# A reciprocal and the low halves of m go ahead of block 0's products by denominators, and block 3's rows are loaded later

## The chip, the cores and the metric

The kernel runs on one core of a Trainium2 chip. A core has five engines, each with its own instruction queue, and an engine works through its queue strictly in the order in which the program was written: TensorE (PE) multiplies matrices and loads their weights (PEld), VectorE (DVE) and ScalarE (ACT) work elementwise, GpSimd (POOL) and SyncE (SP) mostly issue DMA transfers. An instruction that waits holds up everything behind it on its engine. The metric is the device time of one execution in microseconds (us).

## The reference

A transformer block on x of 2048 x 512 in float32, with a condition c that gives six vectors (shift, scale and gate for each half):

```python
mod = (_silu(c) @ w_mod)                 # sa, ca, ga, sb, cb, gb
h = layernorm(x) * (1 + ca) + sa
q, k, v = h @ wqkv                       # 32 heads of 16 columns
pq, pk = phi(q), phi(k)                  # phi(t) = (t > 0 ? t + 1 : exp(t)) + 1e-6
kv = einsum("bhsd,bhse->bhde", pk, v);  z = sum of pk over the rows
o = einsum(pq, kv) / (einsum(pq, z) + 1e-6)
x = x + ga * (o @ wo)
h = layernorm(x) * (1 + cb) + sb
x = x + gb * (mish(h @ w1 + b1) @ w2)    # 512 -> 1792 -> 512
```

## The kernel before, in words

The 2048 rows are cut into four blocks of 512, and a 512-wide dimension into four groups of 128 partitions. A product keeps float32 accuracy by splitting each operand into a high half (rounded, written `...h`) and a low half (the rest, `...l`); `mm3` then issues three matmuls, high x high, high x low, low x high. `split` makes the halves: ScalarE copies the high half, and one step later VectorE subtracts it to get the low half.

The part that the change touches lies at 120 to 200 us. There the keys are done, and the kernel makes q for blocks 2 and 3 and the attention output of all blocks:

- `q_unit(b, g)` multiplies 12 matmuls for group g of block b; `phi` then runs exp and relu on ScalarE and one combining instruction on VectorE (line 374).
- `attend(b, wait, ...)` is a generator that divides q of block b by its denominators. Step one: 16 small matmuls give the denominators (`den_b`, line 948). Step two: VectorE adds a constant and takes the reciprocal (`rden_b`, lines 952 and 953), and a DMA queue writes it to DRAM and reads it back spread over the partitions (`rd_b_0` to `rd_b_3`, lines 955 and 959; for blocks 0 and 1 from POOL's queue, for 2 and 3 from SP's). Then `wait` empty steps. Then, for two pairs of groups, VectorE multiplies q by `rd` (line 967), ScalarE makes the high half, and a step later VectorE makes the low half: `qs_b_gh` and `qs_b_gl`.
- m is the 512 x 512 product of kv and wo, as four products `m_ps_k` whose halves are `m_kh` and `m_kl`.
- `o_unit(b, t)` multiplies 12 matmuls: for g = 0 to 3 the halves of `qs_b_g` with those of `m_g`; `o_post` (line 987) adds the result to the rows of x that `load_x(b, t, "r")` fetched from SP's queue.
- `mod_side` loads columns of the modulation weights (`wm_i`, on SP) and three steps later reduces each on VectorE (line 254). SP also loads pieces of w1 and w2 (`w1p`, `w2p`) and stores prepared operands of w2 (`w2t`) for the second half of the kernel.

The order is set by the code alone here. Side work is spawned as a generator, and `tick()` runs one step of each spawned generator, in the order in which they were spawned. `tick()` is called once after each unit of TensorE, so that a step's instructions stand in the engines' queues behind that unit. From about 194 us on a planner with estimated costs sets the order of the second half of the kernel. Tiles come from one pool of 93 buffers; a load waits until the last reader of the buffer's former tile is done.

## Time and profile before

| | |
|---|---|
| median of three executions | 479.73 us |
| lowest, highest | 479.22, 481.56 us |
| profiled execution, its own time | 481.74 us |
| span of the profile, first to last instruction | 480.0 us |
| mean granted TensorE clock | 0.996 |
| busy: TensorE, VectorE, ScalarE, GpSimd | 470.1, 419.8, 325.6, 150.4 us |

The profiled execution is one of its own, with 1.7 us of its time outside the span. A row of the timeline gives start, duration, engine, line, operation, output <- inputs and the count; in brackets the time for which the engine stood idle before it and what released it. Names in the trace lack block numbers: `qs_2h` is group 2, and the block follows from the time.

### The profile page before, as it was taken

What the parts mean: (1) busy time and instruction counts of PE and PEld (TensorE: products, weight loads), DVE (VectorE), ACT (ScalarE), POOL (GpSimd) and SP (SyncE); (2) the same over time, 40 slices, a digit from 0 to 9 for tenths busy, and PEclk for the clock granted to TensorE, in tenths of its full rate; (3) what the DMA queues carried; (4) which work ended last, traced back from release to release, by engine and by line L of the source; (5) the groups of instructions that cost most, each with busy time, mean ns of one, the idle gap of its engine ahead of it and who ended that gap; (6) DMA issues with size and microseconds to landing.
All of it is one profiled execution on the core that took longest, in us unless ns stands there. A gap on an engine that the chain in (4) does not pass through costs nothing.

```text
span 480.0 us, 7249 instructions
## 1 busy us (share of the span) xinstructions
PE 470.1 (98%) x2292; PEld 385.9 (80%) x2292; DVE 419.8 (87%) x816; ACT 325.6 (68%) x593; POOL 150.4 (31%) x220
## 2 busy tenths in 40 slices
PE   8999999999998999999999999999999999999996
PEld 6788888878876888888888888888888887788886
DVE  6989999898989998998989899989876767999974
ACT  6777686776753998679979898576466657456330
POOL 4583431000022413224342221622131325607330
PEclk9999999999998999999999999999999999999999
DMA  8997699434996466348899542984352469999967
GB/s 308 402 352 213 179 184 269 136 111 133 325 262 165 142 222 215 119 154 273 251 310 320 183 136 83 196 265 133 109 154 66 114 196 231 246 301 191 262 105 131
DMA packets 80480, 97.76 MB, mean 204 GB/s; under 512 B 29521, under 2 KB 53081, under 8 KB 80442
## 3 DMA queue, kind: packets, MB, share of 16 engines
q1 hardware_dynamic: 54376, 57.82, 38.9%
q0 software_dynamic: 22752, 38.43, 32.5%
q10 hardware_dynamic: 3314, 1.05, 1.0%
q8 instruction: 18, 0.29, 0.3%
q14 instruction: 20, 0.16, 0.1%
HBM read 69.22 MB, written 31.99 MB: 211 GB/s over the span
## 4 chain that ended last, share of the span: by engine, by line
PE 88%; DVE 4%; DMA 3%; ACT 2%; issue 1%; POOL 0%; ACTq 0%; POOLq 0%; DVEq 0%
PE p_a L1565 20%; PE pa L1650 11%; PE p_s L1565 8%; PE pc L1650 5%; PE pb L1650 4%; PE pd L1650 4%; PE o L144 3%; PE o L142 3%; PE o L143 3%; PE pq_a L488 3%; PE pk L143 2%; PE gacc L142 2%; PE pk L142 2%; PE pk L144 2%; PE gacc L143 2%; PE gacc L144 2%
## 5 line engine op out<-in xcount | busy, mean ns | idle before, releaser
L1580 ACT ACTIVATE u<-p_a 128x512 f32<-128x512 f32 x42 | 25.0, 596 | 30.3 <-PE p_a L1565 29.7
L1524 POOL DMA_DIRECT2D wt_m<-w2t x32 | 27.9, 1096 | 55.3 <-PE p_a L1565 13.4
L1589 ACT ACTIVATE u_a<-c_a,b1c 128x512 f32<-128x512 f32 x42 | 30.2, 719 | 14.7 <-DVE c_a L1586 12.8
L1715 POOL DMA_DIRECT2D out_dram<-turned x20 | 23.3, 1719 | 36.2 <-DVE turned L1703 24.6
L1586 DVE TENSOR_TENSOR c_a<-p_s,u 128x512 f32<-128x512 f32 x28 | 19.3, 689 | 15.5 <-PE p_s L1565 8.0
L1539 DVE TENSOR_TENSOR u_a<-u_a,u_a 128x512 f32<-128x512 f32 x28 | 18.6, 682 | 0.0
L983 POOL DMA_DIRECT2D out_dram<-r x16 | 9.0, 562 | 27.7 <-DVE r L987 14.9
L278 POOL TENSOR_TENSOR rs_n<-rs_n,half 128x1 f32<-128x1 f32 x16 | 10.6, 667 | 19.7 <-DVE rs_n L304 9.8
L955 POOL DMA_DIRECT2D rden_d<-rden x2 | 1.4, 721 | 47.1 <-DVE rden L953 47.1
L1524 POOL DMA_DIRECT2D wt_m<-w2d x13 | 12.8, 1228 | 10.8 <-DVE c_a L1586 5.0
L371 ACT ACTIVATE e_k<-pk 128x512 f32<-128x512 f32 x15 | 8.9, 591 | 10.5 <-PE pk L144 10.4
L1681 ACT ACTIVATE U<-pa,mc 128x512 f32<-128x512 f32 x10 | 6.9, 686 | 11.1 <-PE pa L1650 11.0
L967 DVE SCALAR_TENSOR_TENSOR q<-q,rd 128x512 f32<-128x512 f32 x16 | 10.6, 686 | 3.9 <-DMA rd<-rden_d 3.9
L1586 DVE TENSOR_TENSOR c_a<-p_a,u 128x512 f32<-128x512 f32 x14 | 9.6, 687 | 4.2 <-PE p_a L1565 1.7
L374 DVE SCALAR_TENSOR_TENSOR ku<-e_k,relu_k 128x512 f32<-128x512 f32 x15 | 10.7, 714 | 2.9 <-ACT relu_k L372 2.7
L278 POOL TENSOR_TENSOR rs_x<-rs_x,half 128x1 f32<-128x1 f32 (+1 forms) x10 | 7.9, 792 | 15.8 <-DVE rs_x L273 14.6
L1617 ACT ACTIVATE u_a<-p_a,b1c 128x512 f32<-128x512 f32 x14 | 9.6, 687 | 4.5 <-PE p_a L1565 4.4
L1366 POOL DMA_DIRECT2D w1p<-w1d x13 | 9.9, 764 | 7.9 <-PE p_a L1565 3.5
L374 DVE SCALAR_TENSOR_TENSOR q<-e_q,relu_q 128x512 f32<-128x512 f32 x16 | 10.6, 686 | 0.5 <-ACT relu_q L372 0.5
L254 DVE SCALAR_TENSOR_TENSOR wm<-wm,sc_row 128x512 f32<-128x512 f32 x16 | 10.6, 678 | 0.0
L1342 ACT ACTIVATE l_m_0h<-u_a 128x512 fp32r<-128x512 f32 x12 | 7.5, 623 | 4.1 <-DVE u_a L1539 4.1
L1348 DVE TENSOR_TENSOR l_m_1l<-u_a,l_m_1h 128x512 fp32r<-128x512 f32 x12 | 8.2, 685 | 2.0 <-ACT l_m_1h L1342 2.0
(1446 smaller groups left out, 1879.4 us busy)
## 6 DMA issues: line engine op xcount, KB each, us to landing
wt_m<-w2t POOLq DMA_DIRECT2D x32, 256.0 KB, 4.4
wt_m<-w2t SPq DMA_DIRECT2D x22, 256.0 KB
r<-in_x_dram SPq DMA_DIRECT2D x16, 256.0 KB
out_dram<-r POOLq DMA_DIRECT2D x16, 256.0 KB, 3.3
x<-in_x_dram SPq DMA_DIRECT2D x15, 256.0 KB
wt_m<-w2d SPq DMA_DIRECT2D x15, 256.0 KB
w1d<-in_w_dram SPq DMA_DIRECT2D x4, 896.0 KB
w1p<-w1d SPq DMA_DIRECT2D x13, 256.0 KB
```

What stands on the lines that cost most here:

```text
L142: pe.matmul(o, st[0], mv[0], start=start, stop=False)
L143: pe.matmul(o, st[0], mv[1], start=False, stop=False)
L144: pe.matmul(o, st[1], mv[0], start=False, stop=stop)
L374: dve.scalar_tensor_tensor(dst, e, 1.0, r, op0=ALU.min, op1=ALU.add)
L1524: q.dma_start(f32(v), (w2d if src == "w2d" else w2t)[g][:, :, part, :])
L1539: dve.tensor_tensor(get(d), u, v, op=o)
L1565: pe.matmul(p, st, mv, start=onto is None and c == 0 and i == 0, stop=c == 1 and i == 2, skip_group_check=onto is not None)
L1580: act.activation(t["u", n], t["pa"], AF.Copy)
L1586: dve.tensor_tensor(t[key], t[p], t["u", n], op=ALU.add)
L1589: act.activation(u, t[key], AF.Mish, bias=b1c[:, f:f + 1])
L1650: pe.matmul(o, st[:, cs], mv, start=not onto and n == 0 and k == 0, stop=n == G - 1 and k == 2, skip_group_check=onto)
L1715: q.dma_start(rows_, sq, accum_op=ALU.add)
```

## The change

On VectorE, in the third unit of q for block 2, block 0's products by denominators come later. `attend(0)` has one empty step less, but is spawned one unit later, after m's splits and behind `attend(1)`. Its second pair of products no longer waits a step for the low halves (`join`). `mod_side` takes its first step by hand at the place where it was spawned, so that its loads keep their step, and runs on behind `attend(0)`. The four loads of block 3's rows go from the units of q for block 2 to the output units of block 0.

```diff
-    def attend(b, wait, queue=pool):
+    def attend(b, wait, queue=pool, join=False):
...
             next(parts[-1])
             if g % 2:
-                yield
+                if g == 1 or not join:
+                    yield
                 run(parts.pop(0))
                 run(parts.pop(0))
...
-    attending = attend(0, 3)
+    attending = attend(0, 2, join=True)
     next(attending)
...
     for g in range(4):
         q_unit(2, g)
-        if g == 1:
-            spawn(attending)
         if g == 2:
             spawn(attend(1, 4))
         if g == 1:
-            spawn(mod_side(range(12, 16), 1))
-        load_x(3, g, "r")
+            mods = mod_side(range(12, 16), 1)
+            next(mods)
         if g == 2:
             for k in range(4):
                 m_ps = ps("acc", f"m_ps_{k}")
                 mm3(m_ps, [h[:, P * k:P * (k + 1)] for h in kvs[0]], wos[k], True, True)
                 spawn(split(f"m_{k}", m_ps, ms, k))
+            spawn(attending)
+            spawn(mods)
         tick()
...
             for t in range(4):
+                load_x(3, t, "r")
                 o_unit(0, t)
```

The first place is VectorE's queue around `rden_1`, from the last of the `mod` columns on. `q_b_g` is q of block b and group g. Before:

```order
L967 SCALAR_TENSOR_TENSOR q_0_0_1380<-q_0_0_1380,rd_0_0_1631 128x512
L967 SCALAR_TENSOR_TENSOR q_0_1_1406<-q_0_1_1406,rd_0_1_1633 128x512
L374 SCALAR_TENSOR_TENSOR q_2_2_1727<-e_q_2_2_1756,relu_q_2_2_1757 128x512
L952 TENSOR_SCALAR rden_1_1819<-den_1_1760,tiny_den_525 128x128
L953 RECIPROCAL rden_1_1819<-rden_1_1819 128x128
L156 TENSOR_TENSOR m_0l_1778<-m_ps_0_1730,m_0h_1777 128x512
L156 TENSOR_TENSOR m_1l_1781<-m_ps_1_1734,m_1h_1780 128x512
L156 TENSOR_TENSOR m_2l_1784<-m_ps_2_1738,m_2h_1783 128x512
L156 TENSOR_TENSOR m_3l_1787<-m_ps_3_1742,m_3h_1786 128x512
L156 TENSOR_TENSOR qs_0_0l_1810<-q_0_0_1380,qs_0_0h_1809 128x512
L156 TENSOR_TENSOR qs_0_1l_1814<-q_0_1_1406,qs_0_1h_1813 128x512
```

And the same place in the changed kernel:

```order
L374 SCALAR_TENSOR_TENSOR q_2_2_1723<-e_q_2_2_1748,relu_q_2_2_1749 128x512
L952 TENSOR_SCALAR rden_1_1801<-den_1_1752,tiny_den_525 128x128
L953 RECIPROCAL rden_1_1801<-rden_1_1801 128x128
L156 TENSOR_TENSOR m_0l_1770<-m_ps_0_1724,m_0h_1769 128x512
L156 TENSOR_TENSOR m_1l_1773<-m_ps_1_1728,m_1h_1772 128x512
L156 TENSOR_TENSOR m_2l_1776<-m_ps_2_1732,m_2h_1775 128x512
L156 TENSOR_TENSOR m_3l_1779<-m_ps_3_1736,m_3h_1778 128x512
L967 SCALAR_TENSOR_TENSOR q_0_0_1380<-q_0_0_1380,rd_0_0_1631 128x512
L967 SCALAR_TENSOR_TENSOR q_0_1_1406<-q_0_1_1406,rd_0_1_1633 128x512
L156 TENSOR_TENSOR qs_0_0l_1820<-q_0_0_1380,qs_0_0h_1819 128x512
L156 TENSOR_TENSOR qs_0_1l_1824<-q_0_1_1406,qs_0_1h_1823 128x512
```

The first two products moved behind seven instructions that use no `rd`. The second place follows directly on VectorE, with the second pair of products. Before:

```order
L967 SCALAR_TENSOR_TENSOR q_0_2_1474<-q_0_2_1474,rd_0_2_1635 128x512
L967 SCALAR_TENSOR_TENSOR q_0_3_1481<-q_0_3_1481,rd_0_3_1637 128x512
L254 SCALAR_TENSOR_TENSOR wm_12_1712,mc_147<-wm_12_1712,sc_row_148 128x512
L374 SCALAR_TENSOR_TENSOR q_2_3_1802<-e_q_2_3_1836,relu_q_2_3_1837 128x512
L156 TENSOR_TENSOR qs_0_2l_1862<-q_0_2_1474,qs_0_2h_1861 128x512
L156 TENSOR_TENSOR qs_0_3l_1866<-q_0_3_1481,qs_0_3h_1865 128x512
```

And in the changed kernel:

```order
L967 SCALAR_TENSOR_TENSOR q_0_2_1474<-q_0_2_1474,rd_0_2_1635 128x512
L967 SCALAR_TENSOR_TENSOR q_0_3_1481<-q_0_3_1481,rd_0_3_1637 128x512
L156 TENSOR_TENSOR qs_0_2l_1862<-q_0_2_1474,qs_0_2h_1861 128x512
L156 TENSOR_TENSOR qs_0_3l_1866<-q_0_3_1481,qs_0_3h_1865 128x512
L254 SCALAR_TENSOR_TENSOR wm_12_1698,mc_147<-wm_12_1698,sc_row_148 128x512
L374 SCALAR_TENSOR_TENSOR q_2_3_1796<-e_q_2_3_1828,relu_q_2_3_1829 128x512
```

The low halves now stand directly behind their products, and `wm_12` and `q_2_3` behind them. On ScalarE only one row moves: the copy `gb_row` (4 x 128) goes from behind `qs_0_3h` to ahead of `qs_0_2h`. TensorE's and POOL's orders stay as they were. The third place is SP's queue, which loads block 3's rows (`r_3_t`). Before, they stand between the loads of `wm_17` and `wm_14`:

```order
L167 DMA r_3_0_1659<-in_x_dram 128x512
L178 DMA wm_18_1661<-wmd_68 128x512
L178 DMA wm_19_1663<-wmd_68 128x512
L167 DMA r_3_1_1700<-in_x_dram 128x512
L178 DMA wm_12_1712<-wmd_68 128x512
L167 DMA r_3_2_1728<-in_x_dram 128x512
L843 DMA w2t_3_1748<-t0_3h_1639 128x512
L843 DMA w2t_3_1748<-t0_3l_1640 128x512
L843 DMA w2t_3_1748<-t1_3h_1642 128x512
L843 DMA w2t_3_1748<-t1_3l_1643 128x512
L178 DMA wm_13_1754<-wmd_68 128x512
L167 DMA r_3_3_1803<-in_x_dram 128x512
```

In the changed kernel they are gone from there and stand here:

```order
L178 DMA wm_15_1870<-wmd_68 128x512
L167 DMA r_3_0_1898<-in_x_dram 128x512
L852 DMA w1p_1_0_1916<-w1d_526 128x4x128
L852 DMA w1p_1_1_1917<-w1d_526 128x4x128
L167 DMA r_3_1_1920<-in_x_dram 128x512
L167 DMA r_3_2_1969<-in_x_dram 128x512
L955 DMA rden_d_2_2004<-rden_2_2001 4x32x128
L959 DMA rd_2_0_2006<-rden_d_2_2004 128x1x512
L959 DMA rd_2_1_2008<-rden_d_2_2004 128x1x512
L959 DMA rd_2_2_2010<-rden_d_2_2004 128x1x512
L959 DMA rd_2_3_2012<-rden_d_2_2004 128x1x512
L167 DMA r_3_3_2015<-in_x_dram 128x512
```

So three of them moved to either side of the `w1p` loads, ahead of `rden_2`'s store, and the last behind block 2's `rd`.

## Prediction

> **What bounds the kernel now.** I read the page's busy times first, then the waits of TensorE, then busy time by stage with the granted clock, then the instructions of one stage engine by engine.

> ```profile
> span 480.0 us, 7249 instructions
> PE 470.1 (98%) x2292; PEld 385.9 (80%) x2292; DVE 419.8 (87%) x816; ACT 325.6 (68%) x593; POOL 150.4 (31%) x220
> PE o L144 <- DVE qs_2l L156: 1.0, 1, 1.0
> PE o L142 <- ACT qs_2h L150: 0.6, 1, 0.6
> ```

> TensorE is the bound: it is busy for 98% of the span. So a change gains only where TensorE stands still or runs slowly. The list of its waits is short, and two of its longest belong to one product: o(0,0), the first output product of block 0, waits for the high and then for the low half of `qs_2`. Does it also cost clock? The next table shows two stretches of 3.41 us there, and a later one in which TensorE also stands still for about a microsecond (first column the stretch, last three the granted clock, the share of DMA and its GB/s).

> ```profile
> core 0: us, PE busy (x) PEld busy (x) DVE busy (x) ACT busy (x) POOL busy (x), PEclk, DMA share, GB/s
> 148.10:151.51 3.41, 1.77 (x7) 1.01 (x7) 3.41 (x8) 3.29 (x7) 1.57 (x3) 1.00 0.09 11
> 151.51:154.92 3.41, 3.41 (x10) 2.64 (x9) 3.41 (x10) 0.01 (x1) 1.32 (x3) 0.50 0.90 220
> 407.50:410.92 3.42, 2.47 (x12) 1.77 (x10) 3.42 (x7) 3.34 (x7) 0.00 (x0) 1.00 1.23 273
> ```

> TensorE is busy for only 1.77 of 3.41 us (52%) in the stretch with the waits, and the stretch after it runs at a clock of 0.50. Around 409 us it was busy for 72% of such a stretch, and the clock stayed at 1.00. So the stall is paid twice: as idle time, and as half speed behind it. Its exact price stands in TensorE's instructions:

> ```profile
> 147.90 0.39 PE L144 MATMUL o<-m_1h,qs_1l 128*128 128x512 f32 x1
> 148.90 0.50 PE L142 MATMUL o<-m_2h,qs_2h 128*128 128x512 f32 x1 [0.61 <-ACT qs_2h L150]
> 150.66 0.50 PE L144 MATMUL o<-m_2h,qs_2l 128*128 128x512 f32 x1 [1.02 <-DVE qs_2l L156]
> 155.81 0.39 PE L144 MATMUL o<-m_3h,qs_3l 128*128 128x512 f32 x1
> 160.01 0.39 PE L142 MATMUL o<-m_0h,qs_0h 128*128 128x512 f32 x1
> 162.50 0.39 PE L144 MATMUL o<-m_3h,qs_3l 128*128 128x512 f32 x1
> ```

> From the start at 147.90 to the start at 155.81 lie 18 matmuls (the rest of o(0,0), 6, and all 12 of o(0,1)). An undisturbed product of 12 matmuls, o(0,3), goes from 160.01 to 162.50 in 11 steps, 0.227 us each. 18 steps are 4.09 us; 7.91 us passed. The loss is **3.82 us**. The half clock is 3.41 x 0.5 = 1.71 us of it; the waits are the other **2.11 us**.

> Why are the halves of `qs_2` late? VectorE tells it:

> ```profile
> 138.41 0.17 DVE L258 TENSOR_SCALAR mc<-mc 128x4 f32<-128x4 f32 x1
> 140.60 0.69 DVE L967 SCALAR_TENSOR_TENSOR q<-q,rd 128x512 f32<-128x512 f32 x1 [2.03 <-DMA rd<-rden_d]
> 141.50 0.69 DVE L967 SCALAR_TENSOR_TENSOR q<-q,rd 128x512 f32<-128x512 f32 x1 [0.21 <-DMA rd<-rden_d]
> 142.12 0.68 DVE L374 SCALAR_TENSOR_TENSOR q<-e_q,relu_q 128x512 f32<-128x512 f32 x1
> 142.72 0.34 DVE L952 TENSOR_SCALAR rden<-den,tiny_den 128x128 f32<-128x128 f32 x1
> 143.97 0.63 DVE L156 TENSOR_TENSOR m_0l<-m_ps,m_0h 128x512 fp32r<-128x512 f32 x1
> 146.30 0.68 DVE L156 TENSOR_TENSOR qs_0l<-q,qs_0h 128x512 fp32r<-128x512 f32 x1
> 147.50 1.28 DVE L967 SCALAR_TENSOR_TENSOR q<-q,rd 128x512 f32<-128x512 f32 x2
> 148.71 0.68 DVE L254 SCALAR_TENSOR_TENSOR wm<-wm,sc_row 128x512 f32<-128x512 f32 x1
> 149.92 0.68 DVE L156 TENSOR_TENSOR qs_2l<-q,qs_2h 128x512 fp32r<-128x512 f32 x1
> ```

> VectorE has no idle time before any row from 142.12 to 149.92, but ahead of that it stands still for 2.03 + 0.21 = 2.24 us, waiting for the denominators that a DMA spreads, while seven instructions that need no denominator (`q_2_2`, two for `rden_1`, four low halves of m) are queued behind. Later two instructions that block 0 doesn't need (`wm`, `q_2_3`) stand between the products and `qs_2l`.

> **The change, part by part.** (1) On VectorE the seven instructions go ahead of the products; nothing is added. Where their inputs come from:

> ```profile
> 137.29 1.08 PE L948 MATMUL den<-q,hmask 128*32 128x128 f32 x32
> 134.77 0.59 ACT L372 ACTIVATE relu_q<-pq 128x512 f32<-128x512 f32 x1
> 137.40 0.60 ACT L150 ACTIVATE m_3h<-m_ps 128x512 fp32r<-128x512 f32 x1
> 141.39 0.63 ACT L150 ACTIVATE qs_0h<-q 128x512 fp32r<-128x512 f32 x1 [3.40 <-DVE q L967]
> 148.22 0.63 ACT L150 ACTIVATE qs_2h<-q 128x512 fp32r<-128x512 f32 x1 [4.38 <-DVE q L967]
> L959 POOL DMA_DIRECT2D rd<-rden_d x4: 604/613/636, 133.6 to 135.4; - x4
> DMA to landing us min/median/max: 7.0/8.1/10.4
> ```

> `den_1` ends at 138.37, the rectified `q_2_2` at 135.36, the last high half of m at 138.00: all are there when VectorE is free at 138.58. The walk through the new order, with the steps of the rows above: `q_2_2` 0.60 to 139.18; `rden_1` and its reciprocal 1.25 (142.72 to 143.97) to 140.43; four low halves 2.33 (143.97 to 146.30) to 142.76. The products then need `rd_0` and `rd_1`, which landed by 140.60 and 141.50: they are hidden, 1.21 for two (147.50 to 148.71), to 143.97. ScalarE starts a high half 0.79 behind its product's start (140.60 to 141.39): `qs_0h` runs 143.55 to 144.18, so VectorE waits some 0.25 us, then two low halves to 145.4, and the second pair of products to 146.65.

> (2) Their low halves follow in the same step. `qs_2h` starts 0.79 behind 145.4, ends at 146.85; `qs_2l` runs from about 146.95 to 147.6, `qs_3l` to 148.2. TensorE, undisturbed, wants them at 147.90 + 0.23 = 148.13 (`qs_2h`), 148.58 (`qs_2l`) and 149.27 (`qs_3l`), and loads weights one step earlier. Margins: 1.0, 0.75 and 0.8 us. So both waits go, and with 100% busy stretches the half clock too: **-3.82 us** at o(0,1)'s end. If the estimate of the chain is wrong by more than 0.75 us, each further microsecond costs one.

> (3) What goes behind: `wm_12` and `q_2_3` come behind `qs_3l`, to start at 148.2 and 148.8, before 148.71 and 149.32. `q_2_3` feeds `den_2`, which TensorE would reach at 156.13 - 3.82 = 152.3: 2.8 us to spare. ScalarE has the exponential and the rectifier of `q_2_3` (0.59 each) between `qs_1h` and `qs_2h`, and now `gb_row` too, a row of four partitions that I take at no more than half of that: from 144.8 it ends at 146.2 at the latest, and `qs_2h` starts at 146.2. All this costs nothing, and what covers it are these margins.

> (4) The four loads of block 3's rows (256 KB each) leave SP's queue among the `wm` loads; three now stand behind `wm_15`, one behind block 2's `rd`. Issue time of those `rd`, and the rows' first reader:

> ```profile
> 163.86 2.89 SPq L959 DMA_DIRECT2D rd<-rden_d  x4
> 199.24 0.68 DVE L1861 TENSOR_TENSOR r<-o,r 128x512 f32<-128x512 f32 x1
> ```

> The latest of the four is so issued near 167, and with the slowest landing above (10.4 us) it is there by 178, 21 us early: nothing. What they stood ahead of on SP comes earlier: the `wm` tiles, four `w2t` stores, the `w2p` and `w1p` loads. These meet the transfer of `rd`. At 273 GB/s, the rate of the stretch at 407 us, where DMA is full, a load takes 0.96 us and four take 3.8. Bounds for the last landing of block 0's `rd`, now 135.4 + 10.4 = 145.8: 3.8 earlier (four loads gone from ahead of it) to 3.8 later (as much brought in). `q_0_3` wants it at 146.05. I take "the same or earlier", since what is removed stood ahead of `rd`, and what comes instead waits for tiles that computation frees. Three of the four also stand ahead of `rden_2`'s store on SP, which issues some 3 us before 163.86; they would have to be 12 us late to hold it up.

> (5) Does the gain last? VectorE gains 2.24 - 0.25 = 2.0 us, TensorE 3.8, so VectorE falls 1.8 us behind. What TensorE asks next:

> ```profile
> 161.70 0.68 DVE L156 TENSOR_TENSOR qs_3l<-q,qs_3h 128x512 fp32r<-128x512 f32 x1
> 162.93 0.69 DVE L987 TENSOR_TENSOR r<-o,r 128x512 f32<-128x512 f32 x1 [0.41 <-PE o L144]
> 168.17 0.39 PE L142 MATMUL o<-m_0h,qs_0h 128*128 128x512 f32 x1
> 171.09 0.69 DVE L987 TENSOR_TENSOR r<-o,r 128x512 f32<-128x512 f32 x1 [0.91 <-PE o L144]
> 181.64 0.68 DVE L156 TENSOR_TENSOR qs_3l<-q,qs_3h 128x512 fp32r<-128x512 f32 x1
> 183.69 0.39 PE L144 MATMUL o<-m_3h,qs_3l 128*128 128x512 f32 x1
> 160.00:180.00 20.00, 20.00 (x116) 16.29 (x115) 17.91 (x40) 18.64 (x38) 5.61 (x10) 1.00 0.65 209
> ```

> Block 1's last half is done at 162.4, and o(1,0) starts at 168.17: 5.8 us of cover for a lag of 1.8. VectorE itself waited 0.41 and 0.91 us for TensorE; those 1.32 us vanish, so by 171 the lag is some 0.5 us. In block 2 the cover is thin: `qs_3l` ends at 182.3, wanted at 183.69, 1.4 us less the weight load; it holds for 0.5 (without it, 0.5 us more to pay). ScalarE is busy for 18.64 us of the 20 from 160 on, so it makes up 1.36 us of the same lag; what is left, some 0.5 us, is inside that cover too. Behind this the order is fixed and whatever waits moves along. I carry -3.8 to the end, with 1 us as the most that may be lost here.

> **The sum.** The profiled execution took 481.74 us (span 480.0): 481.74 - 3.82 = 477.9. But the other executions took 479.22, 479.73 and 481.56. Two of them are 2.0 and 2.5 below the profiled one, one equals it within 0.2: a difference of the size of the half clock (1.71). I read it so: the half clock comes in some executions, not in others, and in the median one it did not come. Then the median loses only the waits: 479.73 - 2.11 = **477.6**, near 477.9. If the median did contain it, 479.73 - 3.82 = 475.9. [...]

> **Rivals.**
> *The half clock has another cause.* For it: a gap of 0.95 us near 409 drew none. Against: 52% busy just ahead of it, and the full clock in the other rows shown. Then the profiled time falls by 2.11 only, to 479.6. [...]
> *Part of the wait stays:* the chain product, high half, low half is longer than my steps by 1.5 us, so `qs_2l` stops TensorE for 0.75 and more. No half clock at 1 us (the stretch at 409). About 478.6.
> *It does nothing:* the wait only goes from `qs_2` to `qs_0`, as the products start 2.2 us later (142.76 against 140.60). Against: `qs_0l` ended at 146.98 before and ends near 144.9 now. 479.7.
> *Slower:* `rd_3` of block 0 lands later, as the brought-forward `w2p`, `wm` and `w1p` loads share its DMA engines, and the second pair of products waits for it with everything else queued behind. From a landing at 146.8 (146.05 plus the margin) it stops TensorE, one to one. With the half clock behind such a stall, it is as dear as the old wait at 146.8 + 3.82 - 1.71 = 148.9, and at my bound, 149.6, it costs 2.8 + 1.71 = 4.5 us where the median before paid 2.11: 482.1. For it: 10.4 us to landing is already the longest of the `rd`. Against: the margins in (4).

> **How the numbers follow.** No change means within 0.5% (2.4 us), about what a measurement can tell here. Waits gone, no half clock in the median before: 0.47, 477.6 (its own range 476.9 to 478.3, so a third of it below 477.33). Waits gone and half clock with them, against the median: 0.31, 475.9. Another cause of the half clock: 0.04, 477.6 to 479.6. Part stays: 0.07. Nothing: 0.05. Slower: 0.06, of it 0.05 beyond 0.5%. Faster by over 0.5%: 0.31 + 0.16 = 0.47; slower 0.05; the rest, 0.48, within. The range goes from 475.5 (the second case with 0.4) to 479.2 (part stays with half a microsecond).

> **What would show it.** Right: `q_2_2`, `rden_1` and m's low halves from 138.6 on without a wait before them; no TensorE wait at `qs_2h` or `qs_2l`; clock 1.00 from 145 to 160; `den_2` near 152.3. Wrong: a DMA wait at the second pair of products; a wait of TensorE at block 2's `qs` that was not there; a half-clock stretch elsewhere; `o` of block 3 waiting for its rows.

## The result, and the profile after

The changed kernel takes 477.99 us (median of nine executions, 477.15 to 479.07), the kernel before, beside it, 480.68 us (nine, 479.22 to 482.38). The ratio is 0.9944 with a 95% interval of 0.9924 to 0.9964: 0.56% faster. The interval leaves out 1, but reaches into the 0.5% that the prediction counts as no change. The profiled execution of the changed kernel took 477.43 us.

The page of the changed kernel, its span, the busy times and the chain of work that ended last; the fourth line is that chain in the kernel before:

```profile
span 475.7 us, 7248 instructions
PE 468.3 (98%) x2292; PEld 385.0 (81%) x2292; DVE 419.8 (88%) x816; ACT 325.1 (68%) x593; POOL 150.6 (32%) x220
PE 93%; DVE 3%; issue 1%; DMA 1%; ACT 1%; POOL 0%; ACTq 0%; DVEq 0%
PE 88%; DVE 4%; DMA 3%; ACT 2%; issue 1%; POOL 0%; ACTq 0%; POOLq 0%; DVEq 0%
```

VectorE does as much as before (419.8 us); TensorE's part of the chain has grown from 88 to 93%: before, the chain ran over DMAs and VectorE from 128 to 151 us, and now it is back on TensorE from 135 us on. TensorE's waits in the changed kernel (engine, line, what was waited for: us in total, times, longest):

```profile
PE warm L213 <- POOL ones L205: 1.1, 1, 1.1
PE tp_x L622 <- ACT x L287: 0.9, 1, 0.9
PE pc L1652 <- DVE l_m_5l L1350: 0.3, 1, 0.3
PE gacc L425 <- POOL pk_2h L152: 0.2, 1, 0.2
```

Both waits at `o` are gone. VectorE's timeline shows the new order (start, duration, engine, line, operation):

```profile
138.80 0.69 DVE L374 SCALAR_TENSOR_TENSOR q<-e_q,relu_q 128x512 f32<-128x512 f32 x1
139.40 0.34 DVE L952 TENSOR_SCALAR rden<-den,tiny_den 128x128 f32<-128x128 f32 x1
139.78 0.95 DVE L953 RECIPROCAL rden<-rden 128x128 f32<-128x128 f32 x1
140.65 0.63 DVE L156 TENSOR_TENSOR m_0l<-m_ps,m_0h 128x512 fp32r<-128x512 f32 x1
...
142.99 1.28 DVE L967 SCALAR_TENSOR_TENSOR q<-q,rd 128x512 f32<-128x512 f32 x2
144.37 0.69 DVE L156 TENSOR_TENSOR qs_0l<-q,qs_0h 128x512 fp32r<-128x512 f32 x1
...
145.58 1.29 DVE L967 SCALAR_TENSOR_TENSOR q<-q,rd 128x512 f32<-128x512 f32 x2
146.96 0.69 DVE L156 TENSOR_TENSOR qs_2l<-q,qs_2h 128x512 fp32r<-128x512 f32 x1
147.57 0.69 DVE L156 TENSOR_TENSOR qs_3l<-q,qs_3h 128x512 fp32r<-128x512 f32 x1
```

No row names a wait (some 0.1 us of idle time is left ahead of `qs_0l` and of `qs_2l`), where the kernel before stood 2.24 us for `rd`. TensorE now runs through the place; this is its timeline, and one stretch of 8 us with the busy time of TensorE, weight loads, VectorE, ScalarE and GpSimd, then the granted clock, the DMA share and GB/s:

```profile
148.44 0.39 PE L142 MATMUL o<-m_2h,qs_2h 128*128 128x512 f32 x1
148.67 0.39 PE L143 MATMUL o<-m_2l,qs_2h 128*128 128x512 f32 x1
148.90 0.39 PE L144 MATMUL o<-m_2h,qs_2l 128*128 128x512 f32 x1
149.12 0.39 PE L142 MATMUL o<-m_3h,qs_3h 128*128 128x512 f32 x1
...
152.62 1.08 PE L948 MATMUL den<-q,hmask 128*32 128x128 f32 x32
148.00:156.00 8.00, 8.00 (x63) 6.36 (x62) 8.00 (x18) 4.17 (x10) 2.97 (x6) 1.00 0.55 145
```

The steps are 0.227 us throughout, the clock is 1.00, and `den_2` comes at 152.62 instead of 156.13.

**Where the time went.** I set the starts of all 2292 matmuls of the two profiled executions side by side. Up to 148 us the changed one is 0.3 us later, from the start of the kernel on. Between 148 and 156 us it gains 3.85 us, and keeps this until 406 us, where another 0.75 us is added at a weight tile of the second half (see the last experiments). In sum 4.31 us, the difference of the two executions' times.

### The profile page after: what moved, and what is told of

Same layout as the page of the kernel before. It is cut to its first block, busy times and chain, and to the rows that moved or that the text cites. A ratio compares the mean times of both kernels' runs of the same rounds, so it can differ in the third digit from the quotient of the medians.

```text
span 475.7 us, 7248 instructions
## 1 busy us (share of the span) xinstructions
PE 468.3 (98%) x2292; PEld 385.0 (81%) x2292; DVE 419.8 (88%) x816; ACT 325.1 (68%) x593; POOL 150.6 (32%) x220
## 4 chain that ended last, share of the span: by engine, by line
PE 93%; DVE 3%; issue 1%; DMA 1%; ACT 1%; POOL 0%; ACTq 0%; DVEq 0%
PE p_a L1567 20%; PE pa L1652 12%; PE p_s L1567 8%; PE pc L1652 5%; PE pb L1652 4%; PE pd L1652 4%; PE o L142 3%; PE o L144 3%; PE o L143 3%; PE pq_a L488 3%; PE gacc L144 2%; PE pk L144 2%; PE gacc L142 2%; PE pk L142 2%; PE gacc L143 2%; PE pk L143 2%
## 5 line engine op out<-in xcount | busy, mean ns | idle before, releaser
L1526 POOL DMA_DIRECT2D wt_m<-w2d x13 | 12.8, 1228 | 10.4 <-DVE c_a L1588 5.0
L371 ACT ACTIVATE e_k<-pk 128x512 f32<-128x512 f32 x15 | 8.9, 591 | 10.5 <-PE pk L144 10.4
L374 DVE SCALAR_TENSOR_TENSOR ku<-e_k,relu_k 128x512 f32<-128x512 f32 x15 | 10.7, 714 | 2.8 <-ACT relu_k L372 2.6
L967 DVE SCALAR_TENSOR_TENSOR q<-q,rd 128x512 f32<-128x512 f32 x16 | 10.5, 686 | 1.5 <-DMA rd<-rden_d 1.5
L374 DVE SCALAR_TENSOR_TENSOR q<-e_q,relu_q 128x512 f32<-128x512 f32 x16 | 10.6, 686 | 0.3 <-ACT relu_q L372 0.3
L254 DVE SCALAR_TENSOR_TENSOR wm<-wm,sc_row 128x512 f32<-128x512 f32 x16 | 10.6, 680 | 0.0
```

The source lines that it names most:

```text
L374: dve.scalar_tensor_tensor(dst, e, 1.0, r, op0=ALU.min, op1=ALU.add)
L1526: q.dma_start(f32(v), (w2d if src == "w2d" else w2t)[g][:, :, part, :])
```

## The experiments

Each kernel ran beside the kernel before on one chip; the medians of the kernel before were 480.34 us on the first of these chips (35 executions; beside the first four kernels), 480.48 on the second (34; the next four) and 479.76 on the third (26; the last three). A ratio stands with its 95% interval. Times of kernels on different chips are compared through these.

### The kernel before, execution by execution

No edit.

> The kernel before, unchanged, to see its executions one by one. My theory: the half clock at o(0,0) comes in some executions and not in others, each costing 1.7 us. Then the nine executions stand in two groups about 2 us apart (some 480.0 and 482.0), and the mean granted clock of the whole span separates them: 1.7 us of loss is 3.4 us at half clock, 0.0036 of the span, so 0.996 to 0.997 with it and 0.998 to 1.000 without. A fresh profile shows either no half clock between 148 and 156 us with a loss of 2.1 us there, or one with 3.8 us. Rivals: the half clock comes in every execution (all times in one group, clock 0.996 throughout, and the change then takes 3.8 us off each); or the spread of the times has another source (two groups, but the clock is the same in both).

Measured: 480.0 us (twelve, 479.12 to 481.39), ratio to the kernel before 0.9986 (0.9966 to 1.0005), which shows how far equal kernels may read apart: 0.3 us. In the fresh profile TensorE waited as in the first one, but had full clock. TensorE's waits, and the stretch of 3.41 us with the two waits and the one behind it, in this execution:

```profile
PE o L144 <- DVE qs_2l L156: 1.0, 1, 1.0
PE o L142 <- ACT qs_2h L150: 0.7, 1, 0.7
148.74:152.16 3.42, 1.86 (x7) 1.25 (x8) 3.42 (x9) 3.16 (x7) 1.40 (x3) 1.00 0.03 5
152.16:155.57 3.41, 3.41 (x39) 2.67 (x41) 3.41 (x10) 0.00 (x0) 1.49 (x3) 1.00 0.99 232
```

Of these twelve, one had a mean clock of 0.995. Of the 95 executions of the kernel before that ran beside all these kernels on the three chips, 22 had a mean clock of 0.994 to 0.996, 4 of 0.997, and 69 of 0.998 to 1.000. The 22 took 481.89 us in the mean, the 69 took 479.92: 1.97 us apart, where the half clock should cost 1.71. So, judged by the mean clock, the half clock comes in a fifth to a quarter of the executions. But the times are not two groups: the 69 alone reach from 477.67 to 483.23 us (standard deviation 1.1 us), so a single time doesn't tell which kind it is. That part of the expectation was wrong.

### Filled waits

```diff
+        filler = ps("h", "filler") if (b, t) == (0, 0) else None
...
+            if filler is not None and g == 2:
+                st, mv = [q[:, ts] for q in qs[b, g]], ms[g]
+                fill(3)
+                pe.matmul(p, st[0], mv[0], start=False, stop=False)
+                pe.matmul(p, st[0], mv[1], start=False, stop=False)
+                fill(5)
+                pe.matmul(p, st[1], mv[0], start=False, stop=False)
+                continue
```

`fill(n)` issues n matmuls on the high halves of `m_0` and `qs_0`, whose result nobody reads.

> The kernel before, with eight extra matmuls of 0.227 us on data that is there, whose result nobody reads: three ahead of the product that waits for qs_2h (0.61 us), five ahead of the one that waits for qs_2l (1.02 us). VectorE and ScalarE work as before, so the low half comes no earlier, but TensorE is busy while it waits. The eight take 1.82 us, the two waits took 1.63 with 0.48 more behind. My theory, that the idle share alone draws the half clock: none between 148 and 156 us in any execution, o(0,1) ends as in the kernel before without the half clock, or a few tenths later; where the kernel before had the half clock the time falls by 1.7 us, elsewhere 0 to 0.3 us more. Median 479.5 to 480.5. Rival, the half clock has another cause at that place (block 0's first product of new data, or something outside): it stays in a part of the executions, and the times stay in two groups 2 us apart.

Measured: 480.1 us (478.81 to 481.40), ratio 0.9985 (0.9964 to 1.0006), all twelve clocks 0.998 to 1.000. The time is that of the kernel before without its half clock (480.01 us in the mean of the 26 such executions on this chip), as expected. By chance none of twelve would show it in 4 of 100 such trials if a share of 22 in 95 held, so alone this is a hint, no proof; the experiment with one gap settles it.

### Only the joined step

```diff
-    attending = attend(0, 3)
+    attending = attend(0, 3, join=True)
```

> Of the change, only this: the low halves qs_2l and qs_3l follow their products at once, ahead of wm and q_2_3. The seven instructions stay behind the products, and the loads stay. By the steps of the profile: two VectorE instructions fewer ahead of qs_2l (0.60 + 0.61 us), less about 0.2 us in which it waits for the high half: qs_2l ends near 149.6 where it ended at 150.6. TensorE wants it at 148.6, so a wait of about 0.8 us stays at qs_2l, 0.2 to 0.4 us with the weight load and qs_3l. The stretch of 3.41 us is then over 70% busy, as was the one near 409 us that kept full clock. My theory: a loss of 0.8 to 1.2 us, no half clock, so about 1 us faster than the kernel before where that had no half clock, 2.7 where it had: median 478.8 to 479.4. Rival A (any idle time here draws the half clock): half the gain, 2.7 us of loss in some executions. Rival B (the place in the queue isn't what counts, the product's late start is): the wait stays at 1.6 us.

Measured: 479.74 us (478.21 to 480.99), ratio 0.9981 (0.9960 to 1.0001), clocks 0.998 to 1.000. TensorE's waits between 140 and 200 us:

```profile
PE o L142 <- ACT qs_2h L150: 0.7, 1, 0.7
PE tp_n L1035 <- ACT n L287: 0.3, 1, 0.3
```

By the starts of the matmuls 1.2 us are lost at the products with `qs_2` where the kernel before, profiled again, loses 2.3, so 1 us is gained there as expected (the wait for `qs_2h` stays, that for `qs_2l` falls to 0.3). But 0.7 us are given back at `tp_n` near 185 us: VectorE is as late as before, TensorE is not, and the lag shows there. So little is left: 0.3 us against the same kernel run once more, which is not a difference.

### Only the loads

```diff
-        load_x(3, g, "r")        # in the units of q for block 2
...
+                load_x(3, t, "r")   # in the output units of block 0
```

> Of the change, only the loads: block 3's rows go behind the output units of block 0; the order on VectorE is as before. In the trace of the changed kernel rd_0 to rd_3 landed at 139.0, 140.7, 141.8, 142.9 where they had landed at 140.6, 141.5, 143.7, 145.8. My theory: VectorE's wait for rd_0 shrinks from 2.0 to 0.4-0.8 us, so everything behind it comes 1.2 to 1.6 us earlier, qs_2l too, and TensorE's waits at o(0,0) shrink from 2.1 us to 0.5-0.9; no half clock. So the loads alone bring 1.2 to 1.6 us (plus 1.7 where the half clock was): median 478.4 to 479.0. Rival, that of the prediction (the loads do nothing for rd, and the earlier landing is due to rd being issued 1.2 us earlier): rd_0 lands at 140 or later, the wait stays 1.5 us or more, and the time is that of the kernel before.

Measured: 478.29 us (477.15 to 479.46), ratio 0.9961 (0.9939 to 0.9982), clocks 0.998 to 1.000. The loads alone take the wait away. VectorE's timeline with the old order:

```profile
138.80 1.36 DVE L967 SCALAR_TENSOR_TENSOR q<-q,rd 128x512 f32<-128x512 f32 x2
140.08 0.68 DVE L374 SCALAR_TENSOR_TENSOR q<-e_q,relu_q 128x512 f32<-128x512 f32 x1
140.68 0.34 DVE L952 TENSOR_SCALAR rden<-den,tiny_den 128x128 f32<-128x128 f32 x1
...
147.88 0.69 DVE L156 TENSOR_TENSOR qs_2l<-q,qs_2h 128x512 fp32r<-128x512 f32 x1
```

`rd_0` landed at 137.8 us by the trace's landings (140.6 before), so the first product starts at 138.80 instead of 140.60, and `qs_2l` starts 2.0 us earlier than in the kernel before (147.88 against 149.92) and ends just in time: TensorE has no wait at `o`. The gain, about 2 us, is more than the 1.2 to 1.6 us expected; the rival (loads do nothing for `rd`) is out. The larger part of the 2.8 us is gained before `rd` is even issued: the store of `rden_0`, behind which it is issued, landed at 131.40 instead of 133.05 us, so `rd_0` was issued at 131.97 instead of 133.62. This holds over all profiles of this document. In the six with the loads moved `rd_0` was issued at 131.97 to 132.94 us and the last `rd` landed at 141.75 to 143.18; in the seven with the loads at the old place the times are 133.39 to 134.02 and 144.52 to 147.21.

### Only the order on VectorE

```diff
-    attending = attend(0, 3)
+    attending = attend(0, 2)
...
-        if g == 1:
-            spawn(attending)
         if g == 2:
             spawn(attend(1, 4))
         if g == 1:
-            spawn(mod_side(range(12, 16), 1))
+            mods = mod_side(range(12, 16), 1)
+            next(mods)
...
+            spawn(attending)
+            spawn(mods)
```

> The change without the joined step: the seven instructions (q_2_2, rden_1 with its reciprocal, m's low halves) go ahead of block 0's products and the loads go later, but qs_2l and qs_3l come a step later, behind wm and q_2_3. From the trace of the changed kernel, where qs_2l ran 146.96 to 147.57: two instructions of 0.6 us more put its end at 148.8 and that of qs_3l at 149.4. TensorE, shifted by 0.3 us in that trace, wants them at 148.6-148.9 and 149.3-149.6. My theory: a remaining wait of 0 to 0.5 us, no half clock, so nearly the whole gain: 478.0 to 478.5. Rival: the joined step carries the gain and the order alone changes little, because the products start 2 us later: a wait of 1 us or more at qs_2l, 479 or more.

Against what this text says, the loads are not moved in the kernel that ran: block 3's rows are loaded at the old place. So it is the order alone. Measured: 477.96 us (477.24 to 479.21), ratio 0.9951 (0.9933 to 0.9969), clocks 0.998 to 1.000, no wait in the list of TensorE's between 140 and 160 us. VectorE, and the weight load of the matmul that takes `qs_2l`:

```profile
143.37 1.28 DVE L967 SCALAR_TENSOR_TENSOR q<-q,rd 128x512 f32<-128x512 f32 x2
...
147.22 0.68 DVE L254 SCALAR_TENSOR_TENSOR wm<-wm,sc_row 128x512 f32<-128x512 f32 x1
147.84 0.68 DVE L374 SCALAR_TENSOR_TENSOR q<-e_q,relu_q 128x512 f32<-128x512 f32 x1
148.44 0.68 DVE L156 TENSOR_TENSOR qs_2l<-q,qs_2h 128x512 fp32r<-128x512 f32 x1
...
149.18 0.19 PEld L144 LDWEIGHTS o<-m_2h,qs_2l 128*128 128x128 f32 x1 [0.20 <-DVE qs_2l L156]
```

With `wm` and `q_2_3` ahead of it, `qs_2l` ends at 149.12. TensorE is 0.34 us later in this execution than in that of the changed kernel, so its matmul is due at 148.90 + 0.34 = 149.24, and its weight load one step earlier. The weight load does wait, by the row, but the matmul starts at 149.24 as it was due, and those behind it 0.07 us late. So `qs_2l` comes just in time, without a margin, and the order alone brings the whole gain.

### Order and joined step, loads at the old place

> The change without its moved loads: block 3's rows are loaded at the old place, the order on VectorE and the joined step are those of the change. My prediction was that the loads do nothing for the gain: rd_2 and rd_3 would land by 145.8 and are wanted by 145.6 to 146.0, with 0.75 us of margin at qs_2l. Theory: the same as the change within 0.3 us (477.7 to 478.3), no TensorE wait above 0.3 us at o(0,0). Rival: in the trace of the changed kernel the rd landed up to 2.9 us earlier than before; if that was due to the loads, rd_3 lands at 145.8 here, the second pair of products waits some 0.3 us for it, and of a slower landing each microsecond beyond 0.75 reaches TensorE: 478.5 to 480.

The edit is the change without its two lines on `load_x`. Measured: 477.91 us (476.62 to 479.19), ratio 0.9953 (0.9934 to 0.9971): that of the changed kernel. The last `rd` landed at 144.5 us (142.9 in the changed kernel), ahead of the 146.05 at which it is read. So beside the new order neither the loads nor the joined step add anything that can be measured in the time. The trace of this kernel shows one small loss that the changed kernel's trace lacks: 0.4 us at `tp_n` near 184 us.

### A late chain: three and six additions

```diff
         parts = []
+        if b == 0:
+            idle = sb("idle")
+            for _ in range(3):           # 6 in the second kernel
+                dve.tensor_tensor(idle, kv, kv, op=ALU.add)
         for g in range(4):
```

> The changed kernel with three extra VectorE additions of 0.6 us ahead of block 0's first products; their result is not used. They make everything behind them on VectorE 1.8 us later, less the wait of 0.1 to 0.3 us that stood there. Tests the margin of 0.75 us at qs_2l that the prediction gave, and whether the wait of the kernel before was only lateness on VectorE. Theory: qs_2l ends at 149.3 where TensorE wants it at 148.6 to 148.9; a wait of 0.6 to 1.1 us at o(0,0), no half clock (the stretch stays over 70% busy); 478.6 to 479.1, and one late chain of 1.8 us on VectorE is not paid again later. Rival A (a larger margin): no wait, time as the change. Rival B (VectorE is itself the bound behind this place): +1.8 us or more, at later waits.

Measured: 479.43 us (478.79 to 480.92), ratio 0.9986 (0.9966 to 1.0006), clocks 0.998 to 1.000. TensorE's waits between 140 and 200 us:

```profile
PE o L142 <- ACT qs_2h L150: 0.5, 1, 0.5
PE tp_n L1039 <- ACT n L287: 0.3, 1, 0.3
```

By the matmuls' starts 1.1 us are lost at o(0,0). The three additions took 2.05 us in the trace (142.68 to 144.73), so about 1.0 us was covered: the margin is a little larger than 0.75, and it ends at `qs_2h`, not at `qs_2l`. Another 0.65 us is lost at `tp_n` near 185 us. That a late chain isn't paid again was wrong, and with it the upper end of the range.

> The changed kernel with six extra VectorE additions of 0.6 us ahead of block 0's first products; their result is not used. VectorE is 3.6 us later there. Theory: TensorE waits 2.4 to 2.9 us at o(0,0), a stretch of 3.41 us is then about as idle as in the profiled kernel before (52% busy or less), and the half clock comes back in some or all executions: 480.4 to 480.9 without it, 482.1 to 482.6 with it, in two groups 1.7 us apart if it depends on where a window falls. Rival (the half clock had another cause than the wait): the clock stays at 1.00 there in all executions, 480.4 to 480.9.

Measured: 481.45 us (480.89 to 483.09), ratio 1.0025 (1.0008 to 1.0041), and no half clock in any of twelve executions (0.998 to 1.000), though TensorE stood longer than in the kernel before:

```profile
PE o L142 <- ACT qs_0h L150: 1.4, 1, 1.4
PE o L142 <- ACT qs_2h L150: 0.7, 1, 0.7
145.46:148.87 3.41, 2.43 (x11) 1.66 (x9) 3.31 (x6) 0.27 (x1) 1.13 (x2) 1.00 0.66 170
148.87:152.29 3.42, 2.28 (x8) 1.26 (x8) 3.17 (x6) 3.11 (x7) 1.78 (x4) 1.00 0.93 217
```

My theory predicted the half clock, and it didn't come; the time is the rival's, some tenths more. The rows show one difference from the kernel before: the first wait begins at 147.89 and the second ends at 151.94, 4.05 us apart, so no stretch of 3.41 us holds both. The idlest stretch of this length at this place, wherever it is laid between 145 and 158 us, has TensorE busy for 1.93 us, where it was 1.77 ahead of the half clock. That this is the reason was not shown.

### One gap

```diff
                 if g == 1 or not join:
                     yield
+                if (b, g) == (0, 3):
+                    idle = sb("idle")
+                    for _ in range(7):
+                        dve.tensor_tensor(idle, kv, kv, op=ALU.add)
                 run(parts.pop(0))
```

> The changed kernel with seven extra VectorE additions of 0.6 us, whose result is not used, directly ahead of qs_2l: TensorE then stands once, for one gap of about 3.3 us (4.2 us less the 0.75 to 1.0 us of margin), instead of twice. Asks what draws the half clock. In ten profiles so far the time at full clock is a whole number of stretches of 3.413 us (43, 137, 138 or 139), counted from a point near 5 us that differs from execution to execution; the half clock stood behind a stretch with TensorE busy for 1.77 us and not behind stretches with 1.86 (the kernel before, again) or 2.28 (six additions). Theory: such fixed stretches, each judged by its own idle share. A gap of 3.3 us in one piece leaves at least 2.0 us idle in one stretch for about 70% of the positions, so the half clock comes in 6 to 10 of 12 executions; mean granted clock 0.994 to 0.997 in those, times in two groups, 481.3 and 483.0 us. Rival A: the total of the wait counts, not its share of a stretch: six additions cost more in two waits than this and drew none, so none here either. Rival B: something outside the kernel draws it in a fifth of the executions: 1 to 4 of 12.

Measured: 483.07 us (482.60 to 485.10), ratio 1.0061 (1.0042 to 1.0080), mean clock 0.992 to 0.996 in all twelve executions. TensorE's wait, the stretch that holds it, and the next:

```profile
PE o L144 <- DVE qs_2l L156: 3.5, 1, 3.5
148.36:151.77 3.41, 0.32 (x2) 0.00 (x0) 3.27 (x6) 0.84 (x2) 1.98 (x4) 1.00 0.84 206
151.77:155.19 3.42, 3.04 (x7) 2.46 (x8) 3.42 (x9) 0.00 (x0) 0.00 (x0) 0.50 0.58 112
```

Of the explanations, the idle share of one stretch of 3.41 us goes with these runs at o(0,0): not the total of the waits (2.1 us with six additions drew no half clock, 1.6 us in the kernel before did), not the longest single wait (1.0 us in the kernel before drew it, 1.4 with six additions and 1.8 with three, at 409 us, did not), and not something outside (a quarter of the executions there, twelve of twelve here). The wait of 1.8 us speaks against it: TensorE was busy for 1.61 us of the stretch that holds it, and the clock stayed at 1.00 (last section). So the runs show no limit of this share. The 70% of the expectation rests on an assumption of the author's, that the half clock comes when TensorE is busy for less than about 1.4 us of a stretch; no run shows that figure, and for a gap of 3.3 us the positions in fact give nearer 80%. With 1.8 us in its place, an estimate between the 1.77 us of the kernel before (half clock) and the 1.86 of the same kernel again (none), every position of a gap of 3.5 us has at least one stretch below it, and twelve of twelve were seen; for the kernel before the same estimate gives about a third of the positions, and a quarter was seen.

### A weight tile of the second half

In all profiles TensorE waits for one weight tile at 406 to 412 us, from nothing to 1.8 us. Three of them (the matmul that waited, in the kernel before, the order alone, three additions):

```profile
410.87 0.47 PE L1650 MATMUL pa<-l_m_1h,wt_m 128*128 128x512 f32 x1 [0.95 <-ACT l_m_5h L1342]
```

```profile
408.34 0.47 PE L1652 MATMUL pa<-l_m_1h,wt_m 128*128 128x512 f32 x1 [1.52 <-DMA wt_m<-w2d]
```

```profile
409.66 0.47 PE L1656 MATMUL pa<-l_m_1h,wt_m 128*128 128x512 f32 x1 [1.83 <-DMA wt_m<-w2d]
```

The first row names ScalarE, whose `l_m_5h` is not an operand of this matmul; the tile is. GpSimd's and SP's queues in the changed kernel (DMA issues) show why it is late:

```profile
394.58 3.29 POOL L1717 DMA_DIRECT2D out_dram<-turned  x3 [8.47 <-DVE turned L1705]
396.62 1.87 POOL L1526 DMA_DIRECT2D wt_m<-w2d  x1
```

```profile
385.91 10.82 SPq L1526 DMA_DIRECT2D wt_m<-w2d  x10
```

GpSimd's queue stands for 8.47 us behind three stores that wait for VectorE, and the tile is behind them. SP's queue issues its neighbours from 385.9 on. The edit sends this one tile there:

```diff
-        yield dma_(load, [("r", L, name, g)], [(src, g, name)])
+        yield dma_(load, [("r", L, name, g)], [(src, g, name)],
+                   queue=SP if (L, name, g) == (2, "m1", 1) else ANY)
```

> The changed kernel, and one load more moved: the second weight tile of the second half's first product (wt_m<-w2d, wanted near 406 us) goes to SP's queue. In all profiles TensorE waited 0 to 1.8 us for it at 406 us: on GpSimd's queue it stands behind three transfers out_dram<-turned that wait for VectorE until 394.6, is issued at 396.6 and lands near 406; SP issues the loads around it from 386 on. Theory: that wait goes in all executions; it was 0.3 us in the changed kernel's profile and 0.9 to 1.8 in three of its variants, so the mean falls by 0.5 to 1 us (median 477.0 to 477.6) and the spread narrows. Rival: the loads share the DMA engines, which are full there, and the tile that is served later is waited for instead: no change, or the wait moves to the next weight tiles at 408 to 414 us.

Measured, on the changed kernel: 477.02 us (nine, 476.53 to 478.75), ratio to the kernel before 0.9934 (0.9910 to 0.9958). The matmuls there run without a gap:

```profile
405.56 0.39 PE L1652 MATMUL pa<-l_m_0h,wt_m 128*128 128x512 f32 x1
405.79 0.39 PE L1652 MATMUL pa<-l_m_1h,wt_m 128*128 128x512 f32 x1
```

> The kernel before with only the weight tile of the second half on SP's queue. If the wait at 406 to 410 us is independent of block 0's chain, the gain is that of the same edit on the changed kernel, 0.5 to 1 us: median 479.2 to 479.8, and the half clock at o(0,0) stays in about a fifth of the executions (clock 0.997 and less). If the gain there is larger than on the changed kernel, part of the changed kernel's gain was this wait.

Measured, on the kernel before: 478.58 us (477.78 to 480.79), ratio 0.9969 (0.9946 to 0.9992): 1.2 us, a little more than expected. Its executions without the half clock took 478.72 us in the mean, against 479.74 for those of the kernel before on this chip. One of twelve had the half clock, the profiled one, and TensorE was busy for 1.72 us of the stretch before it:

```profile
147.92:151.34 3.42, 1.72 (x7) 0.82 (x6) 3.42 (x7) 2.82 (x7) 1.25 (x3) 1.00 0.06 17
151.34:154.75 3.41, 3.41 (x10) 2.65 (x9) 3.41 (x9) 0.48 (x2) 1.63 (x3) 0.50 0.83 242
```

So on the kernel before the tile is a wait of its own, about 1 us in the mean. Changed kernel and tile together gave the lowest median of all, 477.02 us, as much below the 477.99 of the changed kernel; but the two were not run on one chip, and the intervals of their ratios to the kernel before overlap, so that gain is likely and not shown. The spread of the executions did not narrow (standard deviation 0.74 us), so it has another source, which stays open.

## Why the prediction was right

The time, 477.99 us, is 0.4 us above the 477.6 predicted and inside the likeliest case's own range. By its steps:

**What bounds it, and the loss of 3.82 us.** Right, and the split into waits (2.11) and half clock (1.71) nearly so: the profiled executions differ by 3.85 us at this place, and the kernel before, profiled again without the half clock, loses 2.3 us there. "The half clock comes in some executions, not in others, and in the median one it did not come" holds: 22 to 26 of 95, and 1 of 12. With that share the mean should fall by 2.11 + 0.23 x 1.71 = 2.5 us; the means of the nine and nine executions, 480.75 and 478.04, differ by 2.7.

**(1) and (2), the walk on VectorE.** Right within 0.3 us: the second products, predicted from 145.4 to 146.65, ran from 145.58 to 146.87, and `qs_2l`, predicted at 146.95, started at 146.96, in an execution that is 0.3 us later from its start on. The wait of 0.25 us between the pairs became 0.1 us. The margin of 0.75 us was about 1.0, by the additions. But the prediction took both the new order and the joined step as needed, and the joined step is not: with the order alone `qs_2l` is just in time.

**(3).** Right: `den_2` at 152.62 (152.3), `gb_row` took 0.25 us on ScalarE and delayed nothing.

**(4), the loads.** "The same or earlier" was right for `rd`: the last one landed at 142.9 us instead of 145.8. The bounds took the issue of `rd` as it was, until 135.4 us; in the changed kernel it is issued 1.2 us earlier, since the store ahead of it lands earlier. What the prediction did not see is that the moved loads alone would have sufficed: it costed the moved loads at nothing, since the new order hides `rd` anyway. Beside the new order that is so; alone the loads take away the same 2.1 us. The two parts of the change are two cures for one wait, and their gains don't add up.

**(5), whether the gain lasts.** Right in that nothing was lost: no TensorE wait between 140 and 200 us. The place was wrong: I looked at block 2's `qs` near 182 us, and the kernels in which VectorE stays late (joined step alone, additions) pay 0.65 to 0.7 us at `tp_n` near 185 to 188 us. In the changed kernel no wait shows there, so its lag was small enough by then.

**The sum.** The likeliest case came. Its base of 479.73 us, the median of three executions, was up to 0.95 us low against the later medians of 479.76 to 480.68; so the closeness of 477.6 to 477.99 is in part luck: beside the changed kernel the base was 0.95 us higher than taken, the fall was 2.69 us instead of 2.11, and the two misses partly cancel. The profiled pair falls by 4.31 instead of 3.82: 0.75 of it comes from the weight tile, which the prediction took for a gap that stays, less 0.3 lost at the kernel's start.

**The rivals.** Half clock of another cause: out, by the one gap (twelve of twelve) and the filled waits (none of twelve). Part stays, nothing, slower by `rd_3`: none came; the `rd` landed earlier. The full clock behind the gap of 0.95 us near 410, the row that spoke for another cause, agrees with what was measured at o(0,0): TensorE was busy for 2.47 us of that stretch, and the clock also stayed at 1.00 behind one with 1.86 us (the kernel before, again).

## What to carry to other kernels

Where an engine stands in front of a transfer with ready work queued behind it, look at both ends: the ready work can go first, and other loads that are under way beside the transfer can go later; either may be enough, so test each alone before adding their gains. Short waits of the bounding engine can cost nearly as much again in clock: here two of 0.6 and 1.0 us within 3.41 us cost 1.7 us on top of some 2.2, in 22 to 26 of 95 executions by their mean clock, so judge a change by many executions and their clocks, not by two profiles. A queue that must wait for one engine's result (here 8.47 us) is a bad place for a load that is wanted soon: look at what stands ahead of a late tile on its own queue.

## What the runs showed of the hardware

**No busy time of a stretch was found that parts the cases.** At o(0,0) the half clock came behind stretches with TensorE busy for 0.32, 1.72 and 1.77 us, and not behind 1.86, 2.28 and 2.43; the gap of 1.8 us, however, left 1.61 us and drew none:

```profile
407.86:411.27 3.41, 1.61 (x7) 1.38 (x8) 3.41 (x7) 0.88 (x2) 1.48 (x3) 1.00 1.13 303
```

The ends of matmuls are modelled: a matmul's row lasts 0.39 or 0.50 us where the steps are 0.227, so each gap adds 0.2 to 0.3 us of busy time, and stretches with two gaps count as busier than they are. Whether that explains the case, or whether weight loads count too (0.82 and 1.01 us where the half clock came, 1.25 and 1.38 where it didn't), stays open.

Nor does the number of matmuls in these rows part them: 2, 7 and 7 where the half clock came, 7, 7, 8 and 11 where it didn't.
